# An attention–MLP–router kernel: the MLP's second product turned to produce rows with the router's columns, and attention with both heads in one operation a step

## Chip, cores and metric

One core of a Trainium2 chip. The metric is the device time of one execution in microseconds (us), the median of several runs. Everything is float32; large matrix products are made of three products of rounded parts (type fp32r in the profile): `hi` is the rounded value, `lo` the rest, and a product is hi·hi + hi·lo + lo·hi.

## What is computed

```python
# attention with a decay per channel; B=4, H=8, S=768, D=48
state = alpha[t] * state + outer(k[t], v[t]);  y[t] = q[t] @ state
x = y as (3072 tokens, 384 channels)
# MLP
h = x @ w_in                  # 384 -> 2048
x = (h - tanh(h)) @ w_out     # 2048 -> 384
# one of 8 experts for each token
e = argmax(x @ w_gate);  p = softmax(x @ w_gate)[e];  s = sigmoid((x @ w_output_gate)[e])
out = p * s * (relu(x @ w1[e]) @ w2[e])        # 384 -> 1024 -> 384
```

## The kernel before

The tokens are cut into 8 blocks (`NBLK`) of 384 (`TB`). Heads are worked on in pairs: a unit is one block of one pair, 4 units (`NP`) in a block, 32 in all, each in 6 chunks (`NC`) of 64 tokens (`CH`). The program has three stages: a prologue with the attention of block 0's four units; a main loop over the 8 blocks, each of 16 steps `f` (`NF`); and the experts.

**The MLP.** Step `f` takes 128 of the 2048 hidden columns. `h_begin`/`h_step` (L345 to L363) make nine matmuls into `psh` (2 buffers), tanh on ACT (L357), the subtraction on DVE (L359, tile `t`), and `gg` hi on ACT (L361) and lo (L362) on POOL in nearly all of block 0, on DVE after it. `x_step` (L367) for the step before follows on PE: nine matmuls whose stationary operand is a 128x128 piece of `w_out` (`ohi`, `olo`) and whose moving operand is `gg` with 384 tokens, so the result lies transposed, channels by tokens, in the three PSUM banks `x0` to `x2`. At a block's end `evac` copies them to SBUF, and `turn_rows` in the next block multiplies these by `idg`, an identity matrix with the 16 columns of the two gates beside it: 9 products in two instructions each (L422, tile `psg`), which give rows of tokens and, summed on DVE, the logits. `route_score`, `route_rank` and `route_send` follow in the next steps.

**Attention.** Four steps carry one unit, spread over the MLP's steps by `ph = f % 4`: score, carry, update and causal mask at 0; the scan over chunks (`chain`), the keys of the next unit and `states` at 1; the queries of the next unit (`prep_q2`), `readout` and `place` at 2; `turn_k` at 3. The two heads of a pair have buffers of their own in mirrored halves: `XA`/`WA` and `XB`/`WB`. Half of X holds the queries, the other half the masked scores; half of W holds the states (two ACT copies of `SS`, L262 and L263), the other the values. So a chunk of a head is read out by one product over all 128 rows (24 instructions a unit, L280 and L281). `place` subtracts (L289) and sends y to `xT` by DMAs (L298).

**Weights of the MLP in block 0.** They are narrowed from 64 bits by three DVE operations a tile (L308, L310, L312) into tiles `w32` with 3 buffers, cast on ACT (L332), and their lo part made on POOL (L333). Each step of block 0 does two tiles (one of w_in and one of w_out), two steps ahead of their use.

**Order.** Until block 0 begins, PE, ACT and POOL run in program order, DVE until block 1 and SP (the DMA queue) until block 2; elsewhere a scheduler orders each engine's instructions. In the prologue DVE works nearly all the time.

Of the kernel before, what the change touches and what calls it, by code (L numbers as in the profile page):

```python
# [22 lines left out]
E = 8  # L23
# [41 lines left out]
def tile_kernel(ctx, tc, aps, outs):  # L65
# [18 lines left out]
    stg = att.enter_context(tc.tile_pool(name="stg", bufs=5, side="right"))  # L84
# [4 lines left out]
    psa = pss.enter_context(tc.tile_pool(name="psa", bufs=3, space=PSUM))  # L89
# [22 lines left out]
    idg = cp.tile([128, KC, GW], F32, name="idg")  # L112
# [4 lines left out]
    ohi = wp.tile([128, NF, DM], F32R, name="ohi")  # L117
    olo = wp.tile([128, NF, DM], F32R, name="olo")

    XA = [ap1.tile([128, TB], F32, name=f"XA{i}") for i in range(2)]  # L120
    XB = [ap1.tile([128, TB], F32, name=f"XB{i}") for i in range(2)]
    WW = NC * D + 16
    WA = [ap1.tile([128, WW], F32, name=f"WA{i}") for i in range(2)]
    WB = [ap1.tile([128, WW], F32, name=f"WB{i}") for i in range(2)]
    GE = [ap1.tile([128, D, NC + 1], F32, name=f"GE{i}") for i in range(2)]
    VZ = [ap1.tile([128, NA, 2, 2 * D], F32, name=f"VZ{i}") for i in range(2)]
    SS = [ap1.tile([128, D, NC + 1], F32, name=f"SS{i}") for i in range(NP)]

    early = [(p, t) for i in range(3) for p, t in ((psx, f"x{i}"), (psa, "at"))] * 3
    early = early[:4 * NP]  # L130

    def bank(name):
        p, tag = early.pop(0) if early else (psa, "at")
        return p.tile([128, 512], F32, tag=tag, name=name)

# [28 lines left out]
    def load_w_v(u):  # L164
        j, p = units[u]
        sp.dma_start(out=WA[u % 2][64:128, 0:NC * D], in_=aps["vw"][j, p, 64:128])
        sp.dma_start(out=WB[u % 2][0:64, 0:NC * D], in_=aps["vw"][j, p, 0:64])

# [23 lines left out]
    def prep_q2(u):  # L192
        s = st[u]
        q, Pc = s["raw"][:, TB:2 * TB], s["Pc"]
        yield dve.tensor_tensor(out=c3(XA[u % 2])[0:D], in0=c3(q)[0:D], in1=Pc[0:D, :, 1:CH + 1], op=ALU.mult)  # L195
        pool.tensor_tensor(out=c3(XB[u % 2])[64:64 + D], in0=c3(q)[64:64 + D], in1=Pc[64:64 + D, :, 1:CH + 1], op=ALU.mult)  # L196

# [18 lines left out]
    def score(u):  # L216
        s = st[u]
        s["sc"] = ps = bank("pss")
        for c in range(NC):
            cs = slice(c * CH, (c + 1) * CH)  # L220
            pe.matmul(ps[64:128, cs], s["kt"][0:D, c], XA[u % 2][0:D, cs], start=True, stop=True)  # L221
            pe.matmul(ps[0:64, cs], s["kt"][64:64 + D, c], XB[u % 2][64:64 + D, cs], start=True, stop=True)

    def causal(u):
        ps = st[u].pop("sc")
        for X, p0 in ((XA, 64), (XB, 0)):
            if p0 == 0 and u in CAU:
                act.copy(X[u % 2][p0:p0 + 64], ps[p0:p0 + 64, 0:TB])
                pool.tensor_tensor(out=c3(X[u % 2][p0:p0 + 64]), in0=c3(X[u % 2][p0:p0 + 64]),
                                   in1=cmask[p0:p0 + 64].unsqueeze(1).to_broadcast([64, NC, CH]), op=ALU.mult)  # L230
                continue
            yield dve.tensor_tensor(
                out=c3(X[u % 2][p0:p0 + 64]), in0=c3(ps[p0:p0 + 64, 0:TB]),
                in1=cmask[p0:p0 + 64].unsqueeze(1).to_broadcast([64, NC, CH]), op=ALU.mult)

    def carry(u):
        j, p = units[u]
        st[u]["pu"] = pu = bank("psu")
        n = NC + 1
        if j % 2 == 0:  # L240
            dve.memset(pu[:, 0:n * D:n], 0.0)
        else:
            act.copy(pu[:, 0:n * D:n], SS[p][:, :, NC])
# [30 lines left out]
    def readout(u):  # L274
        j, p = units[u]
        s = st[u]
        ps = bank("psy")
        for c in range(NC):
            cs = slice(c * CH, (c + 1) * CH)
# [4 lines left out]
        act.copy(y[:, 0], ps[:, 0:TB])  # L284

    def place(u):
        j, p = units[u]
        y, ps = st[u]["y"], st[u]["py"]
        dve.tensor_tensor(out=y[:, 1], in0=ps[:, 0:TB], in1=y[:, 0].bitcast(F32), op=ALU.subtract)  # L289
        if p == 0:  # L290
            xT[j] = xp.tile([128, 2, KC, TB], F32R, tag="xT", name="xT")
        for hh in range(2):
            c0 = (2 * p + hh) * D
            c = c0
            while c < c0 + D:
                n = min(c0 + D - c, 128 - c % 128)
                s0 = 64 * hh + c - c0
                sp.dma_start(out=xT[j][c % 128:c % 128 + n, :, c // 128, :].bitcast(F32), in_=y[s0:s0 + n].bitcast(F32))  # L298
                c += n
        del st[u]  # L300
# [19 lines left out]
    def conv(f, i):  # L320
# [5 lines left out]
        if i == 0:  # L326
            fs = slice(f * 128, (f + 1) * 128)
            w = w.rearrange("p (k c) -> p k c", k=KC)
            hi, lo = whi[:, :, fs], wlo[:, :, fs]
        else:  # L330
            hi, lo = ohi[:, f], olo[:, f]
        act.copy(hi, w)  # L332
        pool.tensor_tensor(out=lo, in0=w, in1=hi.bitcast(F32), op=ALU.subtract)  # L333
        n = 2 * f + i + 5
        if n < 2 * NF:
            load_w(n // 2, n % 2)

# [29 lines left out]
    def x_step(j, f, gg):  # L367
        if f == 0:
            px[j] = [psx.tile([128, 512], F32, tag=f"x{k}", name=f"x{k}") for k in range(KC)]
# [36 lines left out]
    def evac(j):  # L406
        del xT[j]
        x2 = xp.tile([128, 2, KC, TB], F32, tag="xT", name="x2")[:, 0]
        for k in range(KC):
            (dve.tensor_copy if k == 1 else act.copy)(x2[:, k], px[j][k][:, 0:TB])  # L410
        del px[j]
        rt[j] = x2

    def turn_rows(j):
        x2 = rt[j]
        r = rp.tile([128, NA * ROW + 1], F32, tag="r", name="r")[:, 0:NA * ROW].rearrange("p (a c) -> p a c", a=NA)
        lz = rp.tile([128, NA, 2 * E], F32, tag="lz", name="lz")
        pa = []
        for a in range(NA):
            ps = psa.tile([128, 512], F32, tag="at", name="psg")  # L420
            for k in range(KC):
                pe.matmul(ps[:, k * GW:(k + 1) * GW], x2[:, k, a * 128:(a + 1) * 128], idg[:, k], start=True, stop=True)  # L422
            p3 = ps[:, 0:KC * GW].rearrange("p (k g) -> p k g", g=GW)
            dve.tensor_reduce(out=lz[:, a], in_=p3[:, :, 128:GW].rearrange("p k g -> p g k"), axis=AX.X, op=ALU.add)
            pa.append(p3)
        for a in range(NA):
            act.copy(r[:, a, 0:DM].rearrange("p (k g) -> p k g", k=KC), pa[a][:, :, 0:128])
# [67 lines left out]
    def general():  # L495
        with ExitStack() as g:
# [46 lines left out]
            with tc.For_i(0, NT, 128) as i0:  # L543
# [26 lines left out]
                for kc in range(KC):  # L570
                    pe.matmul(pg[:, 0:2 * E], xT2[:, kc], idg[:, kc, 128:GW], start=(kc == 0), stop=(kc == KC - 1))
# [47 lines left out]
    load_w(0, 1)  # L619
    load_w(1, 0)  # L620
# [7 lines left out]
    for i in range(2):  # L628
        pool.memset(VZ[i][64:128, :, 0], 0.0)
        pool.memset(VZ[i][0:64, :, 1], 0.0)  # L630
        for X, p0 in ((XA, 32), (XB, 96)):
            pool.memset(X[i][p0:p0 + 32], 0.0)
        for W, p0 in ((WA, 32), (WB, 96)):
            pool.memset(W[i][p0:p0 + 32, 0:NC * D], 0.0)
            pool.memset(W[i][:, NC * D:WW], 0.0)
# [35 lines left out]
    for u in range(NP):  # L671
        weave(chain(u))
        states(u)
# [24 lines left out]
        if u == 2:  # L698
            load_w(1, 1)
            load_w(2, 0)  # L700
# [17 lines left out]
    for n, (c, w) in enumerate((("w_gate", 128), ("w_ogate", 128 + E))):  # L718
        sp.dma_start(out=idg[:, :, w:w + E], in_=aps[c].rearrange("(k p) e -> p k e", p=128))
# [4 lines left out]
    for k in range(KC):  # L724
        dve.tensor_copy(idg[:, k, 0:128], ident)
    pend = None
    for j in range(NBLK):
# [159 lines left out]
        for f in range(NF):  # L887
# [13 lines left out]
            if j > 0 and f == 2:  # L901
                route_score(j - 1)
            gg = h_step(j, f)
# [7 lines left out]
            elif ph == 1 and live:  # L911
                states(u)
# [20 lines left out]
            if j > 0 and 1 <= f <= (2 if j == 1 else 3):  # L933
                (turn_rows, route_rank, route_send)[f - 1](j - 1)
# [24 lines left out]
    turn_rows(NBLK - 1)  # L959
    second(0, 0, h0)  # L960
    route_score(NBLK - 1)
# [85 lines left out]
def layout(inputs):  # L1047
# [16 lines left out]
    for hh in range(2):  # L1064
# [6 lines left out]
        vw[:, :, 64 - 64 * hh:128 - 64 * hh] = vc  # L1071
# [34 lines left out]
```

## Time and profile before

| | |
|---|---|
| median of 3 runs | 851.24 us (849.42 to 852.53) |
| the profiled execution | 852.43 us, its span 850.6 us |
| PE busy | 799.6 us (94%) |
| DVE busy | 517.1 us (61%) |
| ACT busy | 385.6 us (45%) |
| POOL busy | 247.2 us (29%) |

PE is TensorE's matmuls, DVE, ACT, POOL and SP are VectorE, ScalarE, GpSimd and SyncE; PEld is TensorE's weight load. The profile's span is what the engines' records cover; the execution's own time is 1.8 us longer. By the trace, step 0 of block 0 begins at about 47 us and the blocks end at about 148, 216, 284, 350, 417, 482, 545 and 597 us; the experts take the rest. A busy PE is not PE at its peak: matmuls overlap, and what counts is the distance of one start to the next.

### The profile page before, as it was taken

The numbers are of one execution on the slowest core, as the hardware profiler recorded it, in microseconds if no ns is written. First come the engines' busy times: TensorE is split into PE (matmuls) and PEld (weight loads), VectorE is DVE, ScalarE is ACT, GpSimd is POOL, SyncE is SP. The second block draws the span as 40 slices with busy tenths as digits, with TensorE's granted clock in tenths as the row PEclk, the third lists the DMA queues.
The fourth block names the chain that finished last, engine by engine and source line by source line (L and its number), as shares of the span: only waits on it lengthen the run. The fifth ranks groups of instructions, "written<-read, shape, count | busy, mean of one in ns | idle before, by whom it ended". The sixth has DMA issues, their size and how long they took to land.

```text
span 850.6 us, 15695 instructions
## 1 busy us (share of the span) xinstructions
PE 799.6 (94%) x5968; PEld 743.8 (87%) x5968; DVE 517.1 (61%) x1051; ACT 385.6 (45%) x795; POOL 247.2 (29%) x216
## 2 busy tenths in 40 slices
PE   6787778999999999999999999999999999999995
PEld 4566667989999999999999999999999999999995
DVE  7999999666666666675676564445443334344421
ACT  3545445544554544545544553435344434435431
POOL 6267776021201221020131130012223314424321
PEclk8689879999999999999999999999999999999998
DMA  8666552773222242242242220024345236235400
GB/s 250 167 186 197 168 149 68 236 224 101 74 75 71 65 118 65 57 132 58 58 133 63 57 75 18 15 97 130 108 163 200 84 133 216 86 118 204 154 26 29
DMA packets 59747, 98.46 MB, mean 116 GB/s; under 512 B 19723, under 2 KB 46112, under 8 KB 59664
## 3 DMA queue, kind: packets, MB, share of 16 engines
q1 hardware_dynamic: 56256, 87.91, 34.9%
q0 software_dynamic: 3408, 9.47, 2.9%
q8 instruction: 49, 0.80, 0.4%
q14 instruction: 34, 0.28, 0.1%
HBM read 72.13 MB, written 16.25 MB: 104 GB/s over the span
## 4 chain that ended last, share of the span: by engine, by line
PE 56%; DVE 19%; issue 8%; DMA 8%; ACT 5%; SPq 2%; POOL 2%; another core or an unknown queue 0%; POOLq 0%; DVEq 0%; ACTq 0%
PE x L373 13%; PE psh L351 12%; PE o L862 11%; PE psf L834 11%; DMA raw<-raw 6%; DVE t L359 2%; DVE Ex L174 2%; PE psg L422 2%; DVE w L308 2%; DVE w L310 2%; PE psu L252 2%; DVE XA L195 2%; DVE SS L256 2%; DVE gg L362 2%; PE pss L221 1%
## 5 line engine op out<-in xcount | busy, mean ns | idle before, releaser
L373 PE MATMUL x<-gg,ohi 128*128 128x384 f32 x768 | 217.3, 350 | 7.1 <-POOL gg L362 3.7
L351 PE MATMUL psh<-xT,whi 128*128 128x384 f32 x768 | 208.8, 345 | 15.8 <-DVE t L359 13.4
L351 PEld LDWEIGHTS psh<-xT,whi 128*128 128x128 f32 x768 | 138.8, 191 | 19.2 <-issue 6.8
L373 PEld LDWEIGHTS x<-gg,ohi 128*128 128x128 f32 x768 | 138.6, 190 | 16.9 <-DVE gg L362 4.9
L351 PE MATMUL psh<-xT,wlo 128*128 128x384 f32 x384 | 131.3, 342 | 0.0
L373 PE MATMUL x<-gg,olo 128*128 128x384 f32 x384 | 129.9, 338 | 0.0
L359 DVE TENSOR_TENSOR t<-psh,t 128x384 f32<-128x384 f32 x128 | 70.5, 551 | 74.9 <-ACT t L357 71.7
L862 PE MATMUL o<-hi,hh 128*128 128x384 f32 (+2 forms) x440 | 115.2, 338 | 0.0
L834 PE MATMUL psf<-xe,hi 128*128 128x256 f32 (+6 forms) x432 | 109.3, 338 | 0.0
L361 ACT CAST gg<-t 128x384 fp32r<-128x384 f32 x128 | 65.6, 512 | 73.3 <-DVE t L359 69.3
L840 DVE SCALAR_TENSOR_TENSOR hh<-psf,hh 128x384 fp32r<-128x384 f32 (+3 forms) x96 | 40.9, 447 | 89.8 <-ACT hh L838 89.6
L357 ACT ACTIVATE t<-psh 128x384 f32<-128x384 f32 x128 | 62.1, 485 | 72.2 <-PE psh L351 71.8
L196 POOL TENSOR_TENSOR XB<-raw,P 48x384 f32<-48x384 f32 x32 | 36.5, 1142 | 170.2 <-issue 139.5
L362 DVE TENSOR_TENSOR gg<-t,gg 128x384 fp32r<-128x384 f32 x114 | 63.2, 555 | 36.4 <-ACT gg L361 36.2
L862 PEld LDWEIGHTS o<-hi,hh 128*128 128x128 f32 (+2 forms) x440 | 78.2, 184 | 1.2 <-DVE hh L840 0.2
L834 PEld LDWEIGHTS psf<-xe,hi 128*128 128x128 f32 x432 | 75.8, 188 | 2.7 <-issue 0.3
L862 PE MATMUL o<-lo,hh 128*128 128x384 f32 (+1 forms) x232 | 77.7, 337 | 0.0
L838 ACT ACTIVATE hh<-psf 128x256 fp32r<-128x256 f32 (+6 forms) x72 | 34.8, 484 | 92.4 <-PE psf L834 73.0
L769 POOL TENSOR_TENSOR lo<-s,hi 128x768 fp32r<-128x768 f32 (+1 forms) x24 | 48.9, 2037 | 94.1 <-ACT hi L768 93.3
L351 PEld LDWEIGHTS psh<-xT,wlo 128*128 128x128 f32 x384 | 73.3, 191 | 1.1 <-POOL wlo L333 0.7
L373 PEld LDWEIGHTS x<-gg,olo 128*128 128x128 f32 x384 | 72.7, 189 | 0.1
L834 PE MATMUL psf<-xe,lo 128*128 128x256 f32 (+6 forms) x216 | 71.9, 333 | 0.0
(144 smaller groups left out, 1282.1 us busy)
## 6 DMA issues: line engine op xcount, KB each, us to landing
raw<-raw SPq DMA_DIRECT2D x32, 579.5 KB
wst<-wio SPq DMA_DIRECT2D x32, 384.0 KB
s<-w SPq DMA_DIRECT2D x24, 512.0 KB
s<-w SPq DMA_DIRECT2D x32, 384.0 KB
xT<-y SPq DMA_DIRECT2D x48, 144.0 KB
rows<-blank SPq DMA_DIRECT2D x8, 772.0 KB
VZ<-vn SPq DMA_DIRECT2D x60, 72.0 KB
xs<-rows SPq DMA_DIRECT2D x4, 772.0 KB
```

The lines of the kernel that those rows point to most:

```text
L196: pool.tensor_tensor(out=c3(XB[u % 2])[64:64 + D], in0=c3(q)[64:64 + D], in1=Pc[64:64 + D, :, 1:CH + 1], op=ALU.mult)
L351: pe.matmul(begun[f][:, 0:TB], w[:, kc, fs], xT[j][:, x, kc], start=(kc + n == 0), stop=(kc == KC - 1 and n == 2))
L357: act.activation(out=t, in_=ps[:, 0:TB], func=AF.Tanh)
L359: dve.tensor_tensor(out=g, in0=ps[:, 0:TB], in1=t, op=ALU.subtract)
L361: act.copy(gg[:, 0], g)
L362: (pool if j == 0 and f not in GLD else dve).tensor_tensor(out=gg[:, 1], in0=g, in1=gg[:, 0].bitcast(F32), op=ALU.subtract)
L373: pe.matmul(px[j][k][:, 0:TB], w[:, f, k * 128:(k + 1) * 128], gg[:, gi], start=(f == 0 and n == 0), stop=(f == NF - 1 and n == 2))
L769: (dve, pool)[i % 2].tensor_tensor(out=lo, in0=t, in1=hi.bitcast(F32), op=ALU.subtract)
L834: pe.matmul(ps[:, 0:n], w[:, kc, fs], xe[:, x, kc], start=(i == 0), stop=(i == 3 * KC - 1))
L838: act.activation(out=hh[:, 0:n], in_=ps[:, 0:n], func=AF.Relu)
L840: dve.scalar_tensor_tensor(out=hh[:, o:o + c.stop - c.start], in0=ps[:, c], scalar=0.0, in1=hh[:, c].bitcast(F32), op0=ALU.max, op1=ALU.su ...
L862: pe.matmul(po[q][m][0:p.stop - p.start, 0:DM], hh[:, p], w[:, f], start=(f == 0 and i == 0), stop=(f == NFE - 1 and i == len(parts) - 1))
```

## The change

The second product. `gg` becomes the stationary operand, 128 tokens at a time, and `w_out` the moving one. Each of the three banks then holds rows of 128 tokens, and the 16 columns of `w_out @ [w_gate, w_output_gate]` are appended to `ohi` and `olo`, so a matmul moves 400 columns (`DG`) instead of 384 and the logits come out beside the rows. `turn_rows` and `idg` are gone. The new `gate(f)` makes the 16 columns in each step of block 0: three transposes of the narrowed tile of `w_out` (`pso`), a copy, three products with the gates' weights (`psl`), a cast on ACT and a subtraction on DVE (L358).

Attention. Both heads have the same layout: `X0` (queries), `X1` (masked scores) and `WV` (values) hold head 0 in rows 0 to 63 and head 1 in rows 64 to 127. The queries of both heads are one DVE operation (before: DVE for one, POOL for the other), the mask is one DVE operation (before: two, or, in four units, one on DVE and one on ACT and POOL). `states` is gone: the readout takes the states from `SS` directly, by a product over 48 rows for the states and one over 64 rows for the values, added up in PSUM: 24 products, 48 instructions a unit, on the four 64x64 quarters of the array in turn. The result fills half of each of two banks, and the DMAs to `xT` become twice as many, half as large.

Buffers. PSUM: two banks for `psy` (and `psu`), one bank (before: three) for `pst`, `pss`, `pso`, `psl` and the router. The weights' staging has 4 buffers (before: 5).

```diff
-            pe.matmul(ps[64:128, cs], s["kt"][0:D, c], XA[u % 2][0:D, cs], start=True, stop=True)
-            pe.matmul(ps[0:64, cs], s["kt"][64:64 + D, c], XB[u % 2][64:64 + D, cs], start=True, stop=True)
+            pe.matmul(ps[0:64, cs], s["kt"][0:D, c], X0[u % 2][0:D, cs], start=True, stop=True)
+            pe.matmul(ps[64:128, cs], s["kt"][64:64 + D, c], X0[u % 2][64:64 + D, cs], start=True, stop=True)
...
-            pe.matmul(ps[0:64, cs], WA[u % 2][:, c * D:c * D + 64], XA[u % 2][:, cs], start=True, stop=True)
-            pe.matmul(ps[64:128, cs], WB[u % 2][:, c * D:c * D + 64], XB[u % 2][:, cs], start=True, stop=True)
+        ps = pair("psy")
+        SP, h = SS[p], NC // 2
+        for c in range(h):
+            for x in range(2):
+                for q in range(2):
+                    for hh in range(2):
+                        cc = q * h + c
+                        cs = slice(cc * CH, (cc + 1) * CH)
+                        o = ps[64 * q:64 * q + 64, hh, c * CH:(c + 1) * CH]
+                        if x == 0:
+                            rs = slice(64 * hh, 64 * hh + D)
+                            w, m = SP[rs, :, cc], X0[u % 2][rs, cs]
+                        else:
+                            rs = slice(64 * hh, 64 * hh + CH)
+                            w, m = WV[u % 2][rs, cc * D:cc * D + 64], X1[u % 2][rs, cs]
+                        pe.matmul(o, w, m, start=(c + x == 0), stop=(x == 1), skip_group_check=True)
...
+    def gate(f):
+        w = gates.pop(f)
+        ps = psa.tile([128, 512], F32, tag="at", name="pso")
+        for k in range(KC):
+            pe.transpose(ps[:, k * 128:(k + 1) * 128], w[:, k * 128:(k + 1) * 128], ident)
+        wT = ap1.tile([128, KC, 128], F32, tag="wT", name="wT")
+        act.copy(wT.rearrange("p k c -> p (k c)"), ps[:, 0:DM])
+        ps = psa.tile([128, 512], F32, tag="at", name="psl")
+        for k in range(KC):
+            pe.matmul(ps[:, 0:2 * E], wT[:, k], wg[:, k], start=(k == 0), stop=(k == KC - 1))
+        act.copy(ohi[:, f, DM:DG], ps[:, 0:2 * E])
+        dve.tensor_tensor(out=olo[:, f, DM:DG], in0=ps[:, 0:2 * E], in1=ohi[:, f, DM:DG].bitcast(F32), op=ALU.subtract)
...
-        for k in range(KC):
+        for a in range(NA):
             n = 0
             for gi, w in ((0, ohi), (1, ohi), (0, olo)):
-                pe.matmul(px[j][k][:, 0:TB], w[:, f, k * 128:(k + 1) * 128], gg[:, gi],
+                pe.matmul(px[j][a][:, 0:DG], gg[:, gi, a * 128:(a + 1) * 128], w[:, f],
                           start=(f == 0 and n == 0), stop=(f == NF - 1 and n == 2))
```

How the order of the engines' instructions changes, at two places. First PE at the start of block 3, where the rows of block 2 were made (`psh` and `x` are the MLP's products, `psg` the turning of rows). Before:

```order
L351 MATMUL psh<-xT,whi 128x384 x2
L373 MATMUL x_2338<-gg,ohi 128x384
L422 MATMUL psg<-idg,x_2311 128x144 x2
L373 MATMUL x_2338<-gg,ohi 128x384
L373 MATMUL x_2338<-gg,olo 128x384
L373 MATMUL x_2339<-gg,ohi 128x384 x2
L373 MATMUL x_2339<-gg,olo 128x384
L422 MATMUL psg<-idg,x_2311 128x144
L373 MATMUL x_2340<-gg,ohi 128x384 x2
L373 MATMUL x_2340<-gg,olo 128x384
L422 MATMUL psg<-idg,x_2311 128x144 x6
```

With the change no `psg` is left on PE, in any block. Second, DVE and PE in step 4 of block 0. On DVE (here with what each waits for), from the subtraction of step 3 (`t_883`) to that of step 4 (`t_942`), in the changed kernel:

```order
L381 TENSOR_TENSOR t_883<-psh_873,t_883 128x384
L313 TENSOR_SCALAR w32_904<-wst_765 128x384 [waits DMAHW6_49,Pool_49]
L313 TENSOR_SCALAR w32_906<-wst_769 128x384 [waits DMAHW7_49,PE_49]
L315 SCALAR_TENSOR_TENSOR w32_904<-wst_765,w32_904 128x384 [waits DVE_49]
L315 SCALAR_TENSOR_TENSOR w32_906<-wst_769,w32_906 128x384 [waits DVE_49]
L317 SCALAR_TENSOR_TENSOR w32_904<-wst_765,w32_904 128x384 [waits DVE_49]
L317 SCALAR_TENSOR_TENSOR w32_906<-wst_769,w32_906 128x384 [waits DVE_49]
L358 TENSOR_TENSOR olo_121<-psl_926,ohi_120 128x16 [waits Activation_49]
L381 TENSOR_TENSOR t_942<-psh_932,t_942 128x384
```

Before, the two first operations of each pair (L308) waited for POOL; now the second waits for PE, and the small L358 stands ahead of the step's subtraction. What PE has done by then: the buffer of `w32_906` is the one that `pso` of step 4 read (`w_752`), and in PE's order of the changed kernel that stands here (the first `psh` rows are those of step 5, the `x` rows those of step 3):

```order
L373 MATMUL psh<-xT,whi 128x384 x2
L373 MATMUL psh<-xT,wlo 128x384
L373 MATMUL psh<-xT,whi 128x384 x2
L373 MATMUL psh<-xT,wlo 128x384
L373 MATMUL psh<-xT,whi 128x384 x2
L373 MATMUL psh<-xT,wlo 128x384
L395 MATMUL x_734<-ohi,gg 128x400
L395 MATMUL x_735<-ohi,gg 128x400
L395 MATMUL x_736<-ohi,gg 128x400
L351 MATMUL pso<-cst,w_752 128x128 x3
L245 MATMUL psu<-VZ_131,ktok 64x2x48 x6
```

The transposes come behind the nine products of step 5 and the first three of step 3's `x`, which wait for `gg` of step 3.

## Rows read from the trace of the kernel before

**Rows 1.** Busy time by engine in stretches: start:end, length, PE, PEld, DVE, ACT, POOL, granted clock, DMA.

```profile
0.00:40.00 40.00, 27.04 (x290) 18.49 (x290) 34.95 (x72) 17.37 (x37) 16.66 (x32) 0.79 0.74 203
40.00:147.00 107.00, 84.19 (x594) 70.49 (x594) 103.43 (x160) 50.21 (x113) 79.14 (x65) 0.86 0.53 156
284.00:350.00 66.00, 65.38 (x564) 61.25 (x563) 44.30 (x97) 32.75 (x74) 11.83 (x11) 1.00 0.30 82
```

**Rows 2.** PE's longest waits, 216 to 482 us: total, times, longest one.

```profile
PE x L373 <- ACT gg L361: 0.7, 4, 0.2
```

**Rows 3.** The chain of waits around the end of block 6: start, duration, what.

```profile
541.12 1.56 PE x L373 x9
...
547.88 2.21 PE psg L422 x18
```

**Rows 4.** Timeline of PE at the start of block 3: start, duration, what.

```profile
287.41 1.63 PE L422 MATMUL psg<-idg,x 128*128 128x144 f32 x12
288.78 0.43 PE L351 MATMUL psh<-xT,wlo 128*128 128x384 f32 x1
```

**Rows 5.** Timeline of PE in the experts: nine matmuls of 424 columns, and the next.

```profile
700.60 0.55 PE L834 MATMUL psf<-xe,hi 128*128 128x424 f32 x2
...
702.34 0.52 PE L862 MATMUL o<-hi,hh 128*128 128x384 f32 x2
```

**Rows 6.** Timeline of PE around one readout of block 4 (24 instructions, 403.10 to 403.80).

```profile
402.84 0.34 PE L351 MATMUL psh<-xT,wlo 128*128 128x384 f32 x1
403.10 0.27 PE L280 MATMUL psy<-XA,WA 128*64 128x64 f32 x1
403.11 0.27 PE L281 MATMUL psy<-XB,WB 128*64 128x64 f32 x1
403.21 0.22 PE L280 MATMUL psy<-XA,WA 128*64 128x64 f32 x1
...
403.79 0.22 PE L280 MATMUL psy<-XA,WA 128*64 128x64 f32 x1
```

**Rows 7.** Timeline of the weight loads in the same readout.

```profile
403.16 0.14 PEld L280 LDWEIGHTS psy<-XA,WA 128*64 128x64 f32 x1
403.16 0.14 PEld L281 LDWEIGHTS psy<-XB,WB 128*64 128x64 f32 x1
```

**Rows 8.** Timeline of DVE in block 0, from step 2 to step 6.

```profile
64.33 0.54 DVE L359 TENSOR_TENSOR t<-psh,t 128x384 f32<-128x384 f32 x1
...
65.27 0.61 DVE L308 TENSOR_SCALAR w<-wst 128x384 int32<-128x384 int32 x2
65.80 1.01 DVE L310 SCALAR_TENSOR_TENSOR w<-wst,w 128x384 int32<-128x384 int32 x2
...
67.68 0.54 DVE L359 TENSOR_TENSOR t<-psh,t 128x384 f32<-128x384 f32 x1
...
69.76 1.17 DVE L308 TENSOR_SCALAR w<-wst 128x384 int32<-128x384 int32 x1 [0.92 <-POOL wlo L333]
...
73.54 0.54 DVE L359 TENSOR_TENSOR t<-psh,t 128x384 f32<-128x384 f32 x1
...
76.51 2.17 DVE L308 TENSOR_SCALAR w<-wst 128x384 int32<-128x384 int32 x2
...
86.76 0.17 DVE L189 RECIPROCAL rP<-rP 128x6 f32<-128x6 f32 x1
...
88.40 1.35 DVE L195 TENSOR_TENSOR XA<-raw,P 48x384 f32<-48x384 f32 x1
89.68 0.54 DVE L359 TENSOR_TENSOR t<-psh,t 128x384 f32<-128x384 f32 x1
```

**Rows 9.** Timeline of DVE in the prologue.

```profile
28.50 0.54 DVE L195 TENSOR_TENSOR XA<-raw,P 48x384 f32<-48x384 f32 x1
...
29.67 0.55 DVE L232 TENSOR_TENSOR XB<-pss,cst 64x384 f32<-64x384 f32 x1
...
43.42 1.21 DVE L725 COPY idg<-cst 128x128 f32<-128x128 f32 x3
```

More of the change, by code (lines that the diff above doesn't have):

```diff
@@ L220, in score @@
             cs = slice(c * CH, (c + 1) * CH)
-            pe.matmul(ps[64:128, cs], s["kt"][0:D, c], XA[u % 2][0:D, cs], start=True, stop=True)
-            pe.matmul(ps[0:64, cs], s["kt"][64:64 + D, c], XB[u % 2][64:64 + D, cs], start=True, stop=True)
+            pe.matmul(ps[0:64, cs], s["kt"][0:D, c], X0[u % 2][0:D, cs], start=True, stop=True)
+            pe.matmul(ps[64:128, cs], s["kt"][64:64 + D, c], X0[u % 2][64:64 + D, cs], start=True, stop=True)
     def causal(u):
         ps = st[u].pop("sc")
[L226 to L234, printed above, removed]
+        yield dve.tensor_tensor(out=c3(X1[u % 2]), in0=c3(ps[:, 0:TB]),
+                                in1=cmask.unsqueeze(1).to_broadcast([128, NC, CH]), op=ALU.mult)
     def carry(u):
         j, p = units[u]
-        st[u]["pu"] = pu = bank("psu")
+        st[u]["pu"] = pu = bank("psu") if early else pair("psu")[:, 0]
         n = NC + 1
@@ L242, in carry @@
         else:
-            act.copy(pu[:, 0:n * D:n], SS[p][:, :, NC])
+            act.copy(pu[:, 0:n * D:n], SS[p][:, 0:D, NC])
     def update(u):
@@ L296, in place @@
                 n = min(c0 + D - c, 128 - c % 128)
-                s0 = 64 * hh + c - c0
-                sp.dma_start(out=xT[j][c % 128:c % 128 + n, :, c // 128, :].bitcast(F32), in_=y[s0:s0 + n].bitcast(F32))
+                for q in range(2):
+                    s0 = 64 * q + c - c0
+                    sp.dma_start(out=xT[j][c % 128:c % 128 + n, :, c // 128, q * TB // 2:(q + 1) * TB // 2].bitcast(F32),
+                                 in_=y3[s0:s0 + n, :, hh].bitcast(F32))
                 c += n
@@ L407, in evac @@
         del xT[j]
[L408 to L415, printed above, removed]
         r = rp.tile([128, NA * ROW + 1], F32, tag="r", name="r")[:, 0:NA * ROW].rearrange("p (a c) -> p a c", a=NA)
         lz = rp.tile([128, NA, 2 * E], F32, tag="lz", name="lz")
-        pa = []
         for a in range(NA):
[L420 to L427, printed above, removed]
+            (dve.tensor_copy if a == 1 else act.copy)(r[:, a, 0:DM], px[j][a][:, 0:DM])
+            dve.tensor_copy(lz[:, a], px[j][a][:, DM:DG])
+        del px[j]
         rt[j] = r, lz
@@ L570, in general @@
                 for kc in range(KC):
-                    pe.matmul(pg[:, 0:2 * E], xT2[:, kc], idg[:, kc, 128:GW], start=(kc == 0), stop=(kc == KC - 1))
+                    pe.matmul(pg[:, 0:2 * E], xT2[:, kc], wg[:, kc], start=(kc == 0), stop=(kc == KC - 1))
                 lz = gl.tile([128, 1, 2 * E], F32, name="lz")
@@ L619, in tile_kernel @@
     load_w(0, 1)
+    for c, w in (("w_gate", 0), ("w_ogate", E)):
+        sp.dma_start(out=wg[:, :, w:w + E], in_=aps[c].rearrange("(k p) e -> p k e", p=128))
     load_w(1, 0)
@@ L630, in tile_kernel @@
         pool.memset(VZ[i][0:64, :, 1], 0.0)
[L631 to L635, printed above, removed]
+        pool.memset(WV[i][:, NC * D:WW], 0.0)
+    for p in range(NP):
+        pool.memset(SS[p][:, D:64], 0.0)
     pool.memset(blank[:, 0:DM + 1], 0.0)
@@ L902, in tile_kernel @@
                 route_score(j - 1)
+            if f in gates and j == 0:
+                gate(f)
             gg = h_step(j, f)
```

75 lines of the change are left out of this document (30 added, 45 removed).

## The prediction

> **What bounds the kernel now.** I read the busy times by stretch first. In the six blocks after block 1 TensorE is all: in the stretch from 284 to 350 it is busy 65.4 of 66 us at a granted clock of 1.00 (its upper level, 2.4 GHz), VectorE 44 us, and the stretches from 216 to 482 look the same [rows 1]. The table of waits agrees: in 266 us the largest sum of TensorE's waits is 0.7 us [rows 2]. So in these blocks a matmul added or removed counts in full, and work taken from VectorE, ScalarE or GpSimd counts for nothing. Before 147 us it is the other way round: VectorE is busy 35 of the first 40 us and 103 of the next 107, TensorE 27 and 84 at a granted clock of 0.79 and 0.86 [rows 1]. There VectorE's list counts, and whatever it waits for. The experts are not touched.
>
> **The second product.** Nine matmuls of 384 columns take 1.56 us in the chain [rows 3], 173 ns each; nine of 424 columns begin at 700.60 and the next matmul at 702.34, 193 ns each [rows 5]. So 40 columns cost 20 ns and 16 cost 8.0. A block has 16 x 9 = 144 such matmuls. In the seven blocks that TensorE sets that is 1008 x 8.0 ns = **+8.1 us**. Block 0's 144 (1.2 us) lie in TensorE's idle time.
>
> **The turning of rows.** All 18 instructions of a block cost 2.21 us where they stand in one piece [rows 3]; twelve of them go from 287.41 to 288.78, 1.37 us [rows 4], so 2.05 for eighteen in the blocks that cut them up. Six blocks at 2.05 and two at 2.21 are **-16.7 us**. Nothing can fill that time: VectorE, next in line, has 22 us to spare in each block [rows 1]. The copies that now follow the product (rows and logits, on ScalarE and VectorE) stand where `evac`'s stood; the next block's nine `x` products wait for the first of them as before.
>
> **The readout.** Before, 24 instructions go in pairs, one on either half of the array's columns: 7 to 10 ns between the two, some 57 ns from pair to pair, 0.70 us in all [rows 6]. Each uses all 128 rows. Now there are 48 half as high, in groups of four quarters. If the four run side by side as the two do, twelve groups of 57 ns are 0.70 us again: **0**. If only two do, they are 24 groups, 1.40 us, and 24 readouts in the blocks that TensorE sets cost +16.8. No row shows four at once. What the rows show is that instructions go out 7 to 10 ns apart, four of which are well under 57, and that the weight loads of a pair begin together at 403.16, while the pair of 403.10 is still in flight on the same 128 rows [rows 6, 7]. I take 0, which lies nearer to these, and keep 16.8 for the range. A gain I exclude: a quarter moves the same 64 columns.
>
> The Trainium skill, "TensorE: Matmul & The Clock Gate", Part 3, speaks against this order of quarters: a weight load overlaps a matmul in flight only where its row group is another, and the third and fourth quarter of each group use the row groups of the first and second. The trace does not agree: the loads at 403.16 overlap matmuls on the same rows [rows 7].
>
> **Breaks.** From the last wide matmul to the readout's first take 0.26 us, against 0.17 between wide ones [rows 6, 3]; coming out costs about as much, so a break is 0.18. In the changed order a block's readouts stand in five pieces instead of four: 7 x 0.18 = **+1.3**. The state copies and POOL's query operation cost nothing to drop in these blocks; I give less lateness of `gg` **-1**.
>
> **The prologue.** VectorE loses four mask operations (one of 0.55 a unit) and the `idg` copies, 1.21 us [rows 9]: 3.4. Against this stand twice as many transfers of y on SP's queue, and the next unit's input, which comes by that queue and must be there before VectorE's first scan of it. I take **-3**, with ends of -5 (POOL's removed operations no longer slow VectorE) and 0 (the queue eats it all).
>
> **Block 0.** The steps begin at 64.33, 67.68, 73.54 and, two later, 89.68: 25.35 us for four [rows 8].
> - *Removed.* Beside POOL's work VectorE's operations are longer: two L308 take 2.17 instead of 0.61 [rows 8], the query operation 1.35 instead of 0.54 [rows 8, 9]. POOL loses the two operations (queries, mask) that stand there. 1.5 + 0.8 = 2.3 in four steps.
> - *Added.* L358, a small operation as the one at 86.76: 0.17 in each step. Then the wait of the order's second place. The second narrowing of a step waits for transposes that stand behind nine `psh` and three `x` products, which begin only after the step's subtraction. From one subtraction to the next this is a loop: 0.54 for it, 1.56 for `psh` at the upper clock [rows 3], 0.55 for three `x`, 0.35 for three transposes (as three of `psg`, 114 ns each [rows 4]), 0.2 as my estimate for the two handovers, 0.3 for the late L308, 2.0 for the four operations after it (1.01 a pair), 0.2 for L358: 5.7 us [rows 3, 8]. At the lower clock (1.2 GHz) `psh` takes twice as long: 7.3. Steps of 3.35 and 5.86 grow to that; those of 7 and 9 us have other work to put into the wait. So +2.2 at the one clock, +5.4 at the other; I take the middle, 3.8.
> - *Sum.* +3.8 - 2.3 = 1.5 in four steps. Narrowing goes on for 13 steps: **+5**. The ends: -5 (the scheduler's work hides the wait, only the savings and L358 count: -2.3 + 0.7 = -1.6, times 13/4) and +10 (lower clock throughout: 3.1 times 13/4).
>
> **The sum.** -16.7 + 8.1 + 0 + 1.3 - 1 - 3 + 5 = -6.3. The profiled execution took 852.4, so 846.1; the median of the three lies 1.2 lower, so **845.0 us**. A measurement of this kernel tells about 0.3% (2.6 us) from no change.
>
> **The rivals.**
> 1. *Quarters two at a time.* Place: the 24 readouts between 147 and 540 us. 845 + 16.8 = **862**, slower. It decides from +0.37 us a readout on (6.2 + 2.6 over 24): from 88 instead of 57 ns a group. For it: no row shows four; eight instructions must go out in 57 ns where four do now. Against it: pairs leave 7 to 10 ns apart and loads overlap [rows 6, 7]. 18%.
> 2. *The loop of block 0 at the lower clock.* +10 instead of +5: **850**, the same. For it: the granted clock of 0.86 and VectorE at 103 of 107 us [rows 1]. Against it: where VectorE waits it does nothing that would have to be done twice, and a later step may catch up. 17%.
> 3. *Block 0 gains.* The wait is hidden and only the savings are left, -5: **835**, faster. For it: VectorE already waits 0.92 us for POOL at 69.76 [rows 8], which the new wait may replace. 10%.
> 4. *One bank where there were three.* Keys, scores, transposes and router follow each other in one PSUM bank, each after a copy that empties it, which I put at the 0.54 us of a VectorE operation on such a bank [rows 8]. If TensorE stands for one such handover per unit, 24 x 0.54 = +13: **858**, slower. For it: VectorE's and ScalarE's copies queue behind others. Against it: the scheduler puts 1.56 us of `psh` or `x` between them, and TensorE waits for nothing now [rows 2]. 5%.
>
> **Chances and range.** The forecast has 50%, the rivals 18, 17, 10 and 5. Faster are the forecast (less 3 points for its upper end, where block 0 and the prologue go to their bad sides), rival 3 and a little of rival 2: 60%. The same: most of rival 2 and those 3 points: 17%. Slower: rivals 1 and 4: 23%. The range goes from rival 3 to 858, which takes in rivals 2 and 4 and a readout that loses half of 0.70 us (845 + 8.4 = 853), and leaves out most of rival 1: **835 to 858**. The forecast's own range is 840 to 850.
>
> **What would show it.** In the changed profile: nine `x` matmuls in 1.63 us; no `psg`; a readout of 48 instructions in 0.7 us (1.4 for rival 1); blocks of about 65 us from block 2 on; step 0 of block 0 some 3 us earlier and four steps of it in about 27 us, with VectorE's narrowing idle on TensorE's transposes (rival 3: 24 us and no such wait). I am wrong if readouts are longer than 1 us, if TensorE shows waits for copies of its one bank, or if block 0 ends after 155 us.

## The result, and the profile after

The changed kernel took 856.68 us (median of 7 runs, 854.74 to 862.51), the kernel before 851.3 beside it (849.42 to 854.07): a ratio of 1.0072, 95% interval 1.0048 to 1.0097. It is slower. The range of the forecast holds the time; its direction was wrong.

The execution whose trace was first taken was the longest of the seven (862.51 us), so a second trace of the same kernel is set beside it below (run r1, 858.3 us). Where a stage begins is read from VectorE's subtractions (L359 before, L381 after), sixteen to a block; all in us:

| | to block 0 | block 0 | blocks 1 to 7 | from the last subtraction on | span |
|---|---|---|---|---|---|
| before | 47.8 | 100.2 | 446.0 | 256.7 | 850.6 |
| changed, first trace | 45.7 | 113.4 | 447.2 | 254.4 | 860.7 |
| changed, r1 | 45.6 | 111.1 | 445.4 | 254.5 | 856.5 |
| r1 against before | -2.2 | +10.9 | -0.7 | -2.2 | +5.9 |
| forecast | -3 | +5 | -6.1 | -2.2 | -6.3 |

So two stages went wrong: block 0, and the blocks that TensorE sets. The runs were made on several chips, on which the kernel before takes 851.3 to 854.8 us, and each run has one trace; the same kernel's block 0 took 113.4 and 111.1 us. So I read nothing into differences of block 0 below some 3 us between runs.

Busy times by stretch of the first trace, in the columns of [rows 1]:

```profile
40.00:147.00 107.00, 92.01 (x752) 81.81 (x751) 81.21 (x157) 46.87 (x118) 53.33 (x50) 0.91 0.49 157
284.00:350.00 66.00, 66.00 (x641) 61.86 (x641) 39.06 (x94) 26.10 (x60) 6.26 (x7) 1.00 0.29 82
```

In the second stretch TensorE is as full as before. In the first VectorE has gone from 103 of 107 us to 81: work was taken from it, and yet the block is longer, so it waits. The waits of VectorE, then of TensorE, from 46 to 150 us (total, times, longest):

```profile
DVE w L313 <- PE pso L351: 10.7, 4, 3.7
DVE olo L358 <- ACT ohi L357: 8.7, 10, 2.4
DVE X L226 <- PE pss L222: 2.9, 4, 1.3
```

```profile
PE pso L351 <- DVE olo L358: 9.2, 5, 2.6
PE pss L221 <- DVE olo L358: 4.9, 4, 3.5
```

The forecast saw the first of these five. The second line is the small L358 standing in VectorE's list until ScalarE's cast is done; the last two are TensorE waiting for the one bank, which is free only when L358 has read it. Two signs that the forecast named for being wrong are here: TensorE waits for its one bank, and block 0 ends after 155 us (VectorE's first subtraction of block 1 stands at 159.1 us, in r1 at 156.7). The third, a readout longer than 1 us, comes next. VectorE's timeline shows a step (start, duration, what, and the idle time before it with what ended it):

```profile
69.93 0.55 DVE L381 TENSOR_TENSOR t<-psh,t 128x384 f32<-128x384 f32 x1
70.86 1.15 DVE L313 TENSOR_SCALAR w<-wst 128x384 int32<-128x384 int32 x1 [0.38 <-POOL wlo L339]
73.33 0.36 DVE L313 TENSOR_SCALAR w<-wst 128x384 int32<-128x384 int32 x1 [1.31 <-PE pso L351]
73.61 1.02 DVE L315 SCALAR_TENSOR_TENSOR w<-wst,w 128x384 int32<-128x384 int32 x2
74.55 1.02 DVE L317 SCALAR_TENSOR_TENSOR w<-wst,w 128x384 int32<-128x384 int32 x2
76.06 0.17 DVE L358 TENSOR_TENSOR olo<-psl,ohi 128x16 fp32r<-128x16 f32 x1 [0.49 <-ACT ohi L357]
76.15 0.55 DVE L381 TENSOR_TENSOR t<-psh,t 128x384 f32<-128x384 f32 x1
```

From subtraction to subtraction 6.2 us, with 2.2 us of waits in it. Now a readout in block 3 of the first trace:

```profile
315.89 0.34 PE L395 MATMUL x<-olo,gg 128*128 128x400 f32 x1
316.17 0.47 PE L283 MATMUL psy<-X,SS 48*64 48x64 f32 x8
316.45 0.30 PE L283 MATMUL psy<-X,WV 64*64 64x64 f32 x8
316.56 0.42 PE L283 MATMUL psy<-X,SS 48*64 48x64 f32 x8
316.80 0.30 PE L283 MATMUL psy<-X,WV 64*64 64x64 f32 x8
316.92 0.42 PE L283 MATMUL psy<-X,SS 48*64 48x64 f32 x8
317.15 0.30 PE L283 MATMUL psy<-X,WV 64*64 64x64 f32 x8
317.38 0.63 PE L395 MATMUL x<-ohi,gg 128*128 128x400 f32 x2
```

Read the distances between the starts. Eight instructions with values as weights (`WV`) are followed by the next group after 0.11 to 0.12 us: two groups of four quarters at 56 to 60 ns each, as fast as the pairs of [rows 6] (58 to 59 ns, after a first distance of 107). Eight with states (`SS`) take 0.23 to 0.28: about twice as long. From the first to the last instruction a readout takes 1.07 us in the blocks from 2 on, against 0.70 before (three of a block's four; other products cut the first in two). The weight loads by shape (total us, mean ns of one) show the same:

```profile
L283 PEld LDWEIGHTS psy<-X,SS 48*64 48x64 f32 x768 | 35.8, 202 | 9.7 <-issue 6.9 <-DVE cum L479 1.2 <-DVE y L292 0.6
L283 PEld LDWEIGHTS psy<-X,WV 64*64 64x64 f32 x768 | 27.0, 147 | 0.4 <-issue 0.4
```

The second product came out as priced. In the chain of waits nine `x` products take 1.65 us where nine of 384 columns take 1.56 [rows 3]:

```profile
284.90 1.56 PE psh L373 x9
286.79 1.65 PE x L395 x9
```

The median distance of two `x` products from 228 to 420 us went from 174 to 182 ns, the 8 ns of the forecast.

### The profile page after: what moved, and what is told of

It is laid out like the page before. It is cut to its first block, busy times and chain, and to the rows that moved or that the text cites. A ratio compares the mean times of both kernels' runs of the same rounds, so it can differ in the third digit from the quotient of the medians.

```text
span 860.7 us, 17129 instructions
## 1 busy us (share of the span) xinstructions
PE 821.5 (95%) x6736; PEld 768.1 (89%) x6736; DVE 472.1 (55%) x1036; ACT 341.9 (40%) x735; POOL 188.6 (22%) x174
## 4 chain that ended last, share of the span: by engine, by line
PE 72%; issue 4%; DMA 3%; DVE 3%; ACT 1%; SPq 1%; POOL 1%; POOLq 0%; DVEq 0%; ACTq 0%
PE x L395 21%; PE psh L373 20%; PE o L864 11%; PE psf L836 11%; PE psy L283 3%; PE pss L221 2%; DMA raw<-raw 2%; PE psu L245 2%; PE pst L815 1%; PE pst L212 1%; DMA s<-w 1%; DMA xT<-y 1%; DVE P L186 1%; POOL out L882 1%; DVE t L381 0%
## 5 line engine op out<-in xcount | busy, mean ns | idle before, releaser
L395 PE MATMUL x<-ohi,gg 128*128 128x400 f32 x768 | 218.5, 359 | 1.7 <-ACT gg L383 1.3
L373 PE MATMUL psh<-xT,whi 128*128 128x384 f32 x768 | 206.5, 347 | 2.6 <-DMA xT<-y 2.2
L395 PEld LDWEIGHTS x<-ohi,gg 128*128 128x128 f32 x768 | 139.8, 191 | 7.8 <-ACT gg L383 1.9
L373 PEld LDWEIGHTS psh<-xT,whi 128*128 128x128 f32 x768 | 140.6, 192 | 6.1 <-issue 2.2
L395 PE MATMUL x<-olo,gg 128*128 128x400 f32 x384 | 133.7, 348 | 0.0
L381 DVE TENSOR_TENSOR t<-psh,t 128x384 f32<-128x384 f32 x128 | 71.0, 554 | 110.6 <-ACT t L379 110.5
L192 POOL TENSOR_TENSOR kt<-kh,rP 128x384 f32<-128x384 f32 x32 | 28.3, 884 | 285.7 <-PE pss L222 243.2
L395 PEld LDWEIGHTS x<-olo,gg 128*128 128x128 f32 x384 | 73.3, 191 | 0.1
```

What stands on the lines that cost most here:

```text
L192: pool.tensor_tensor(out=s["kt"], in0=s["kh"], in1=rP.unsqueeze(2).to_broadcast([128, NC, CH]), op=ALU.mult)
L373: pe.matmul(begun[f][:, 0:TB], w[:, kc, fs], xT[j][:, x, kc], start=(kc + n == 0), stop=(kc == KC - 1 and n == 2))
L381: dve.tensor_tensor(out=g, in0=ps[:, 0:TB], in1=t, op=ALU.subtract)
L395: pe.matmul(px[j][a][:, 0:DG], gg[:, gi, a * 128:(a + 1) * 128], w[:, f], start=(f == 0 and n == 0), stop=(f == NF - 1 and n == 2))
```

## The experiments

Each run was timed beside the kernel before on its chip; ratios are against that, with 95% intervals. The theory after reading the trace: **the states are slow weights because the readout takes every seventh element of `SS`** (`SP[rs, :, cc]`), and **block 0 is held by what the router's columns wait for** (three narrowing buffers, one bank, L358 on VectorE). The rivals: quarters of 48 rows or the adding up of two products are slow; something else of the attention lengthens block 0.

**r1, the changed kernel again.**

> The changed kernel once more, as the measure of the others on this chip. Its profile showed 1.1 us for a readout of 48 instructions, block 0 of 113 us and a granted clock of 0.74 in 147 to 160 us. Theory: the readout and block 0 come again; the low clock after block 0 may be of that one execution. Expected 855 to 858 us, ratio to the kernel before 1.005 to 1.010.

858.74 against 854.62, ratio 1.005 (1.0031 to 1.0069); the stages are in the table above. The readout and block 0 came again. In the first trace the granted clock was 0.74 in 147 to 160 us, in r1 it was 0.93, and r1's blocks 1 to 7 were 1.9 us shorter.

**r2, states side by side.**

```diff
-                            w, m = SP[rs, :, cc], X0[u % 2][rs, cs]
+                            w, m = SP.rearrange("p d c -> p (d c)")[rs, cc * 64:cc * 64 + 64], X0[u % 2][rs, cs]
```

> The readout reads 64 states that lie side by side in SS instead of every seventh element; these are the wrong states, so the rows, the routing and with them the experts' time change: only the stages up to 600 us are compared. Theory (the step of seven elements makes the states' weight loads slow): the 48 instructions take 0.7 us instead of 1.1, and blocks 2 to 5 are shorter by 4 x 4 x 0.41 = 6.6 us. Rival (quarters of 48 rows, or the adding up of two products in one PSUM place, are slow): 1.1 us as before, the blocks the same.

Readout 0.71 us; blocks 2 to 5 took 261.4 us instead of 267.2 in r1 (-5.8, expected -6.6). Height and adding up were as before, so they are not the cause. Its weight loads:

```profile
L283 PEld LDWEIGHTS psy<-X,SS 48*64 48x64 f32 x768 | 23.7, 138 | 9.8 <-issue 6.9 <-DVE cum L479 1.2 <-DVE y L292 0.6
```

**r12, the step by size.**

```diff
+                            n = (1, 2, 3, 4)[p]
-                            w, m = SP[rs, :, cc], X0[u % 2][rs, cs]
+                            w, m = SP.rearrange("p d c -> p (d c)")[rs, cc * 32:cc * 32 + 63 * n + 1:n], X0[u % 2][rs, cs]
```

> The readout's states are read with a step of 1, 2, 3 or 4 elements (4, 8, 12, 16 bytes) in the four units of a block in turn, instead of 7 (28 bytes). They are the wrong states, so only the readouts' lengths in blocks 1 to 5 are compared; nothing else is changed. Theory (each element from another 16 bytes costs, as the Trainium skill's page SBUF — State Buffer says of its lines of 16 bytes): steps 1 and 2 take 0.71 us a readout, step 4 takes 1.07 like step 7, step 3 lies between. Rival (any step above 1 costs the same): step 1 takes 0.71, steps 2, 3 and 4 take 1.07.

Timeline of TensorE, a step of 2, of 3 and of 4 elements (8, 12 and 16 bytes), the first two groups of a readout each:

```profile
309.95 0.35 PE L284 MATMUL psy<-X,SS 48*64 48x64 f32 x8
310.12 0.30 PE L284 MATMUL psy<-X,WV 64*64 64x64 f32 x8
...
325.34 0.41 PE L284 MATMUL psy<-X,SS 48*64 48x64 f32 x8
325.57 0.29 PE L284 MATMUL psy<-X,WV 64*64 64x64 f32 x8
...
341.42 0.47 PE L284 MATMUL psy<-X,SS 48*64 48x64 f32 x8
341.71 0.29 PE L284 MATMUL psy<-X,WV 64*64 64x64 f32 x8
```

The first eight instructions, those with states, take 0.17, 0.23 and 0.29 us, the readout 0.735, 0.897 and 1.076. Step 4 costs what step 7 costs, step 2 almost nothing, step 3 half. (The readouts of step 1 were cut in two by other products and give no length.) It is the theory's order, not "any step".

**r4, one state copy back.** ScalarE copies both heads' states into `SC`, where a chunk's lie side by side.

```diff
+    def states(u):
+        act.copy(SC[:, 0:NC * D].rearrange("p (c d) -> p c d", d=D), SS[units[u][1]][:, :, 0:NC].rearrange("p d c -> p c d"))
-                            w, m = SP[rs, :, cc], X0[u % 2][rs, cs]
+                            w, m = SC[rs, cc * D:cc * D + 64], X0[u % 2][rs, cs]
```

> A copy of the states on ScalarE is put back, one for both heads (128x288), into a buffer in which the states of a chunk lie side by side; the readout keeps its four quarters. Theory of the step of seven elements: readout 0.7 us, 24 x 0.41 = -10 us, so 845 to 849 us. Rival (quarters of 48 rows or the adding up): readout 1.1 us, no change or slower by the copies in block 0, 855 to 860 us.

852.11, ratio 0.9974 (0.9955 to 0.9994); 6.6 us less than r1 on the same chip (expected: 10). Readout 0.71, blocks 1 to 7 439.0 us. Its readout, and the next product:

```profile
311.54 0.34 PE L287 MATMUL psy<-X,SC 48*64 48x64 f32 x8
311.71 0.30 PE L287 MATMUL psy<-X,WV 64*64 64x64 f32 x8
311.82 0.30 PE L287 MATMUL psy<-X,SC 48*64 48x64 f32 x8
311.94 0.30 PE L287 MATMUL psy<-X,WV 64*64 64x64 f32 x8
312.06 0.30 PE L287 MATMUL psy<-X,SC 48*64 48x64 f32 x8
312.17 0.30 PE L287 MATMUL psy<-X,WV 64*64 64x64 f32 x8
312.40 0.64 PE L399 MATMUL x<-ohi,gg 128*128 128x400 f32 x2
```

After the first, which takes 0.17, all groups of eight now follow each other at 0.11 to 0.12 us. Four quarters do run side by side. So the copies that the change removed had made the states fit to be read, and no cost of the one put back shows: block 0 stayed at 110.9.

**r7, without the router's columns.** The 16 columns are copies of the tile's first 16, so transposes and products are left out.

```diff
-            gates[f] = w
+            act.copy(ohi[:, f, DM:DG], w[:, 0:2 * E])
+            pool.tensor_tensor(out=olo[:, f, DM:DG], in0=w[:, 0:2 * E], in1=ohi[:, f, DM:DG].bitcast(F32), op=ALU.subtract)
```

> The router's columns are not computed: the 16 columns of each tile are copied from its first 16 (so transposes, products, L353 and L358 are left out, and the routing is another; only the stages up to 600 us are compared). It prices all that the columns cost block 0. Theory: block 0 about 100 us or less, as before the change (-11). Rival (something else in the change, the attention or the rows as moving operand, lengthens block 0): still over 107 us.

Block 0: 95.4 us, 15.7 less than r1; block 1 took 69.0 instead of 64.1, so over both it is 10.9 less. So beside the new attention the columns lengthen block 0; r9 shows what they cost beside the old one.

**r3, four narrowing buffers.**

```diff
-    stg3 = att.enter_context(tc.tile_pool(name="stg3", bufs=3, side="right"))
+    stg3 = att.enter_context(tc.tile_pool(name="stg3", bufs=4, side="right"))
```

> Four buffers instead of three for the narrowed weights, so that the narrowing of a step waits for the transposes of the step before its own. Theory (the loop from the subtraction over the transposes to the narrowing sets block 0): block 0 goes from 113 to about 105 us, the total falls by 5 to 10 us. Rival (the single bank, whose next user waits for L358 at the end of VectorE's list, sets it): VectorE's wait for the transposes goes, block 0 stays within 3 us.

860.01, ratio 1.0074 (1.005 to 1.0098); block 0 110.1. VectorE's wait for the transposes went, that of L358 for ScalarE grew to 17.4 us in ten. The rival came true, and the loop is not the only cause.

**r5, L358 off VectorE.**

```diff
-        act.copy(ohi[:, f, DM:DG], ps[:, 0:2 * E])
-        dve.tensor_tensor(out=olo[:, f, DM:DG], in0=ps[:, 0:2 * E], in1=ohi[:, f, DM:DG].bitcast(F32), op=ALU.subtract)
+        lw = rp.tile([128, 2 * E], F32, tag="lw", name="lw")
+        act.copy(lw, ps[:, 0:2 * E])
+        act.copy(ohi[:, f, DM:DG], lw)
+        pool.tensor_tensor(out=olo[:, f, DM:DG], in0=lw, in1=ohi[:, f, DM:DG].bitcast(F32), op=ALU.subtract)
```

> The router's columns leave their PSUM bank by one ScalarE copy, and the lo part is made on GpSimd from that copy instead of by L358 on VectorE, so that the single bank no longer waits for VectorE's list. Theory (block 0 is set by the single bank: transposes and scores wait for L358 behind the narrowing): block 0 from 111 to about 105 us, TensorE's wait for L358 (9.2 us) gone, total 4 to 8 us lower than the changed kernel. Rival (the loop over the transposes and the three narrowing buffers): block 0 within 2 us of 111, VectorE's wait for the transposes larger than 10 us.

855.11, ratio 1.0044 (1.003 to 1.0058); block 0 106.5. TensorE's wait for L358 went, and VectorE's wait for the transposes took over (46 to 150 us):

```profile
DVE w L313 <- PE pso L351: 15.6, 5, 4.9
```

Block 0 lost 4.6 us, and the other wait grew as the rival said. In the whole time the expected 4 to 8 us did not come: the ratio is that of r1 (1.005) within the intervals, and block 1 took 66.8 us instead of 64.1.

**r6, the edits of r3, r4 and r5 together.**

> Three edits together: the one state copy on ScalarE (readout 0.7 us), the lo part of the router's columns on GpSimd, four narrowing buffers. Theory (states' step of seven, and in block 0 the two waits stand in for each other so that only both edits help): block 0 about 102 us, blocks 2 to 5 about 65 us each, ratio to before 0.985 to 0.992. Rival (TensorE's own work for the router's columns sets block 0): block 0 stays at 108 to 111, ratio 0.997 as with the copy alone.

856.65, ratio 1.0055 (1.0036 to 1.0074). Readout 0.71, but block 0 112.6: a miss for both theories. Scores now stood behind transposes and products in the queue for the bank, and VectorE behind the scores:

```profile
DVE X L227 <- PE pss L223: 19.7, 3, 8.6
```

**r8, r6 with `gate(f)` behind the attention of its step.**

```diff
-            if f in gates and j == 0:
-                gate(f)
             gg = h_step(j, f)
...
+            if f in gates and j == 0:
+                gate(f)
             if pend is not None:
                 x_step(*pend)
```

> As r6 (state copy, lo part on GpSimd, four narrowing buffers), but gate(f) stands behind the step's attention instead of ahead of it, so that scores and their mask are not queued for the one bank behind the transposes and products of the same step. In r6 VectorE stood 19.7 us in three waits for scores, up to 8.6 us, and block 0 took 112.6. Theory (the queue for the one bank): these waits go, block 0 about 103 us, ratio to before 0.987 to 0.992. Rival (TensorE's own 16 us for the columns set it): block 0 stays over 109, ratio over 0.996.

855.09, ratio 1.0004 (0.9986 to 1.0021). Those waits fell to 1.5 us, block 0 to 106.4, not 103. But block 1 took 71.4 us where r4 took 64.5, so over both blocks r8 is no shorter than r4 (177.8 and 175.4). Waits for transposes were back, with four buffers:

```profile
DVE w L317 <- PE pso L355: 12.9, 9, 3.1
```

Each time a wait was taken away, another grew. No edit that kept the one bank and the columns brought block 0 under 106.

**r9, the second product alone.** The attention of before, its 24 instruction readout, its three banks, its two state copies; the rows, the columns and `gate(f)` as in the changed kernel. Against the kernel before, its core:

```diff
-                pe.matmul(px[j][k][:, 0:TB], w[:, f, k * 128:(k + 1) * 128], gg[:, gi],
+                pe.matmul(px[j][a][:, 0:DG], gg[:, gi, a * 128:(a + 1) * 128], w[:, f],
...
+            if f in gates and j == 0:
+                gate(f)
             gg = h_step(j, f)
```

> One part of the change alone: the kernel before with the second product by rows, the router's columns and gate(f), but the attention of before, with its buffers, state copies, 24 instruction readout and three banks. Theory: readout 0.70, blocks 2 to 5 shorter than before by about 0.7 us each (2.05 less 144 x 8.0 ns), the experts' stage 2.2 less; block 0 longer than before by the loop over the transposes (narrowing still has three buffers), but without the single bank's queue: 103 to 107 us. Total 849 to 853 on a chip where before takes 851, ratio 0.997 to 1.003. Rival (the single bank has no part in block 0): block 0 at 111, ratio over 1.003.

847.74 against 854.8: ratio **0.992** (0.9897 to 0.9944), faster than both kernels and than expected. Block 0 103.3, blocks 1 to 7 439.3, readout 0.70. In 216 to 482 us TensorE waits for nothing. From 46 to 150 us VectorE never waits for the transposes, though the narrowing has three buffers as in the changed kernel. In block 0 the chain of waits is mostly VectorE's list, step by step, with ScalarE's casts ahead of L358 (here L353) in some steps. In this step L353 is one row of the list:

```profile
64.14 0.08 DVE olo L353
64.22 0.48 DVE t L376
```

**r10, the attention alone,** with the turning of rows of before. Against the changed kernel, its core:

```diff
-                pe.matmul(px[j][a][:, 0:DG], gg[:, gi, a * 128:(a + 1) * 128], w[:, f],
+                pe.matmul(px[j][k][:, 0:TB], w[:, f, k * 128:(k + 1) * 128], gg[:, gi],
...
-            if f in gates and j == 0:
-                gate(f)
...
-                (route_rank, route_send)[f - 2](j - 1)
+                (turn_rows, route_rank, route_send)[f - 1](j - 1)
```

> The other part alone: the attention of the changed kernel with its quarters, its states read from SS, its two banks for psy and the single bank, but the second product of before with the turning of rows. Theory: block 0 about 95 to 98 us (as with the columns left out), readout 1.07 us, blocks 2 to 5 longer than the changed kernel's by 0.9 each (2.05 less 1.15), that is about 67.5; the experts as before (256.7). Total about 851 to 857 where before takes 851, ratio 1.000 to 1.007. Rival (the attention is what lengthens block 0): block 0 over 105, ratio over 1.012.

868.89 against 853.13: ratio 1.0169 (1.0146 to 1.0192), slower than expected. Block 0 was 93.5 us, 6.7 less than before; but block 1 took 74.3 instead of 65.3, blocks 2 to 5 68.6 each, the last block 54.0 instead of 50.2, and the experts' stage 258.7 instead of 256.7. Where these were lost was not followed up.

**r11, r9 with the edit of r5 (the lo part on GpSimd).**

> r9 (rows and columns alone, ratio 0.992) with the lo part of the router's columns made on GpSimd from a ScalarE copy, so that VectorE no longer waits for ScalarE's cast (5.5 us in eight waits in r9's block 0). Theory (VectorE's list sets block 0 in r9, as the chain of waits says): block 0 from 103.3 to 99 to 101 us, ratio 0.987 to 0.990. Rival (GpSimd's list is as full, and its longer operations slow VectorE): block 0 103 or more, ratio 0.992 or higher.

848.61, ratio 0.9937 (0.9921 to 0.9953); block 0 104.6. A miss, and what the rival said: beside the old attention, taking L358 off VectorE gains nothing.

**Blocks 0 and 1 together.** A block's mark is VectorE's first subtraction, and the changes shift VectorE against TensorE: the first step of block 1 takes 3.1 us before, 0.6 in r1, 5.7 in r7 and 5.5 in r10. So a part of what block 0 shows comes back in block 1 (us):

| | block 0 | block 1 | both |
|---|---|---|---|
| before | 100.2 | 65.3 | 165.4 |
| changed, first trace | 113.4 | 66.3 | 179.7 |
| changed, r1 | 111.1 | 64.1 | 175.2 |
| r4, state copy | 110.9 | 64.5 | 175.4 |
| r5, L358 off VectorE | 106.5 | 66.8 | 173.3 |
| r8 | 106.4 | 71.4 | 177.8 |
| r7, columns left out | 95.4 | 69.0 | 164.3 |
| r9, second product alone | 103.3 | 64.3 | 167.5 |
| r10, attention alone | 93.5 | 74.3 | 167.8 |

## Why the prediction was wrong

**Right.** What bounds each stage; the turning of rows (2.2 us less in the experts' stage, forecast 2.2, and none left in the blocks); 8.0 ns for 16 columns; the prologue's -2.2 (forecast -3). The sum for blocks 1 to 7 without the readout's term was -6.1; r9, which has the old readout, measured -6.8, and r4, with quarters at full speed, -7.1.

**The readout's 0** ("if the four run side by side as the two do, twelve groups of 57 ns are 0.70 us again") is the first step that failed. The condition held: four quarters run side by side, in r4 at 0.71. What the forecast did not look at is how the weights lie. Before, a copy had put a chunk's states side by side; the changed readout takes them 28 bytes apart. That is 0.37 us a readout, and 24 x 0.37 = 8.9; 6.4 us came back in blocks 1 to 7 with r4, 6.1 of them in the sixteen readouts of blocks 2 to 5. With this alone mended the kernel is a little faster than before (0.9974), so this step turned the direction. The 0.37 lies between the ends I gave (0 and 0.70), for a reason that stood in no rival. The Trainium skill, "SBUF — State Buffer", the note on cachelines in Door 1, says that accesses which go to another line of 16 bytes each time pay a penalty, and that at least two in a line are needed for full bandwidth. r12 agrees: 8 bytes 0.735 us, 12 bytes 0.897, 16 bytes 1.076, 28 bytes 1.069. That rule spoke against this change, and I weighed another.

**The rule that I did weigh** (the Trainium skill, "TensorE: Matmul & The Clock Gate", Part 3), that a weight load overlaps matmuls in flight only for another row group, does not hold here as I put it: groups of four quarters, of which two share each row group, follow each other at 56 to 60 ns, and the loads of one group begin while the products of the group before are in flight on the same rows (their ends are modelled by the profile). I left out that the same Part also lets a load run ahead into the background weight buffer. The time of a load still counts: where the loads of states took 64 ns longer in the mean (202 against 138), a group took about 60 ns longer. Rival 1 (862 us) fell with r4.

**Block 0's +5** is the second: +3.8 for what is added less 2.3 for what is removed, in four steps, times 13/4. Neither term came out alone, and they do not add up. The removed side, 7.5 us over 13 steps, shows in block 0 when the attention is changed alone (-6.7), but not over blocks 0 and 1: +2.4 in r10, and -1.1 in r7, which has both parts without the columns. The added side, 3.8 x 13/4 = 12.4, measured 15.7 in block 0 and 10.9 over both blocks beside the new attention (r1 less r7), but only 3.1 and 2.1 beside the old one (r9 against before), where VectorE does not wait for the transposes at all. "L358, a small operation ... 0.17" priced a duration and not a wait, though the order showed one: L358 stood 8.7 us in ten waits for ScalarE, and TensorE waited 14.1 us (9.2 and 4.9) until it had read the bank. But these waits overlap others; with L358 off VectorE the whole time stayed (r5).

The working has two slips. Its +2.2 lets the step of 5.86 us shrink to 5.7; without that it is +2.35. And at the lower clock it doubles `psh` but not the `x` products and the transposes; with them the loop is 8.2 us and the same sum gives +8.

Rival 2 had the size (+10) and the wrong reason: the granted clock was 0.91. Rival 4 had the bank, but in the wrong stage: I placed it in the 24 units where TensorE waits for nothing, and took the absence of waits before, with three banks, as evidence. That the range held the time is in part luck: it allowed for a readout that loses half of 0.70 us, but its upper end was set by rival 4 at a place where nothing of it came.

**What the two parts do to each other.** Against before, the attention alone changes block 0 by -6.7 (r10), the columns alone by +3.1 (r9), both together by +10.9: 14.5 us more than the sum. Over blocks 0 and 1 it is +2.4, +2.1 and +9.8 (first trace +14.3): 5 to 10 us more. In the whole time there is no such excess: against the kernel before on each chip, r9 is 7.1 us shorter, r10 15.8 longer and r1 4.1 longer, less than the sum of 8.7, as r10 loses in later stages what the two together do not. The two parts share the PSUM banks: the new attention takes two for `psy` and leaves one, and the new columns need that one twice a step. That the columns cost more beside the new attention is shown (r7, r9). That the single bank is the reason is argued from the waits only, as r9 brings back the whole attention of before and not its banks alone; how the cost divides between the bank, the narrowing buffers and the order of the instructions stays open: r3, r5, r6 and r8 each moved the wait. A version with the new attention and more banks for the short products was not tried; both kernels allot eight banks in all.

## What to carry to other kernels

Ask of each operand that a change hands directly to TensorE how far apart its elements lie; a copy on an idle engine may have been what made it fast. When a small operation is added to an in-order list, price what it waits for and what its buffer's next user waits for, not its duration alone. Count a stage's gain to the end of the next stage: r8's block 0 was 4.7 us shorter than r1's and its block 1 7.3 us longer. Two changes that draw on one resource (here PSUM banks) are to be timed one at a time: the second product alone was 0.8% faster, the attention alone 1.7% slower.

## What was not expected of the hardware

A load of 64 columns of weights from elements 28 bytes apart took 202 ns in the mean instead of 138 (r2), and a group of four quarters 115 to 120 instead of 56 to 60 ns; a step of 8 bytes cost 3% of a readout (0.735 against 0.712), one of 16 bytes as much as one of 28. Four 64x64 quarters with four sets of weights ran at 56 to 60 ns a group, the pace of two halves.
